# Attention laid between feed-forward matmuls: value products of a tile as one unit, and scores on four quarters of the array

## The chip, the cores and the metric

One core of a Trainium2 chip runs the kernel. The metric is the device time of one execution in microseconds, the median of several runs; lower is better.

## The reference

Three layers, one after the other. Pooled attention: keys and values are averaged over groups of 8 tokens, so each of 576 queries of a batch sees 72 keys. Then a feed-forward layer over 4608 tokens, and a mixture of 8 experts of which each token takes the best one.

```
k_p = k.reshape(B, H, 72, 8, 64).mean(axis=3); v_p likewise      # B = H = 8, D = 64
scores = scale * q @ k_p.T;  attn = exp(scores - max);  attn /= sum + 1e-9
x = (attn @ v_p), as [4608, 512]
h = x @ w_in                                                      # 512 -> 2048
g = h where h >= 1, 0 where h <= -1, else (h + 1)**2 / 4
y = g @ w_out                                                     # 2048 -> 512
e = argmax(y @ w_gate);  out = p_e * relu(y @ w1[e]) @ w2[e]      # 512 -> 1024 -> 512
```

## The kernel before

The order of the work is written out by hand; each engine runs its instructions in the order in which the code issues them.

The 4608 tokens are 36 tiles of 128, in ten blocks of 3, 4 (seven times), 3 and 2 tiles. For each block `j` the feed-forward layer makes 16 steps `m`: `f1(j, m)` (L592 to L594, 12 matmuls into bank `ps0` or `ps1`) computes 128 of the 2048 hidden columns, and `f2(j, m)` (L635 to L637, three matmuls a tile into `ps2` to `ps5`) adds their share to the output. Each product is three matmuls of a high and a low part (hi x hi, hi x lo, lo x hi). `f1` runs two steps ahead of `f2`. Between them the activation goes through DVE (clip, L599), ACT (square, L600), DVE (larger of both, L610), ACT (high part, L611), DVE (low part, L621); the last three are put off to the next `flush()` through the list `later`.

After each `f1` and each `f2` comes a `slot(j, s)`, s = 0 to 31. A slot of block `j` issues the attention of the tiles of block `j + 1`: `run_units` takes about one unit from the list `units`, then `flush()`, then one or two steps from `todo`, the routing of block `j - 1` (its logits are L666 and L672, its counts L697 and L698). To some units a `kv_step` is tied: the sum over 8 tokens of a head's keys or values on DVE (L244).

The units of a tile are listed by `tile_units`, seven of them, and `weave` mixes those of neighbouring tiles. They are: 0 the transposed queries (`u_qt`), 1 and 2 the scores of heads 0 to 3 and 4 to 7 (`u_sc`), 3 and 5 the turning of the probabilities, 4 and 6 the value products of heads 0 to 3 and 4 to 7 (`u_pv`). For tiles 9 to 33 (`turned`) 3 is `u_turn_p`, a transpose on DVE (L383, L385) and a store to `p_d`, and 5 is `u_place_p`, the loads from `p_d` into `PT` (L392); the order is 3, 2, 5, 0 of the next tile, 4, 6. Both banks that units and routing may use are `ps6` and `ps7`, handed out in turn by `bank()`.

`u_sc` computes two heads with one matmul of the whole array (L340): 128 rows are the 64 dimensions of two heads, and the 144 moving columns of `KBD` hold the pooled keys of both with zeros in the off-diagonal blocks. DVE takes the maxima (L347) and subtracts (L357), and after the second half ACT takes the exponential (L360). A tile that straddles two batches (4, 13, 22, 31) does so for 64 tokens at a time, with 64 columns of the array.

`u_pv` computes a head with one matmul (L416; 72 keys are the rows, 64 dimensions the columns, 128 tokens move), two heads for the upper and lower half of a bank. ACT writes the high part to `XT` (L421), DVE the low part (L422); `XT` is what `f1` of the next block streams.

`u_kt(b)` turns the pooled keys of a batch and writes both blocks of `KBD` (L291, L292).

Of the kernel before, what the change touches and what calls it, by code (L numbers as in the profile page):

```python
# [13 lines left out]
ALU = mybir.AluOpType  # L14
# [9 lines left out]
def attention_ffn_routed_experts_kernel(  # L24
# [38 lines left out]
    AHEAD = 2  # L63
    PICK = NB - 4
    TURN0, TURN1 = 9, NTILE - 2
    CHUNK = S // 64

    sb = ctx.enter_context(tc.tile_pool(name="sb", bufs=1))
# [35 lines left out]
    def at(o, n, p=128):  # L104
        return AT[0:p, o:o + n]
# [2 lines left out]
        return FX[:, o:o + n]  # L108

    KBD = [at(576 * i, 576).rearrange("p (a c) -> p a c", a=4) for i in range(2)]  # L110
    QB = [at(1152 + 512 * i, 512) for i in range(2)]
    QT = at(2176, 512)
    SC = [at(2688, 576), at(7616, 576)]
# [100 lines left out]
    def turned(t):  # L214
        return TURN0 <= t < TURN1
# [38 lines left out]
    def bank():  # L254
        banks.rotate(-1)
        return banks[-1]
# [6 lines left out]
    def mix(n=1):  # L263
        for _ in range(min(n, len(pend))):
            pend.popleft()()
# [19 lines left out]
    def u_kt(b):  # L285
        pb = bank()
        for c in range(4):
            nc.tensor.transpose(pb[:, c * SP_:(c + 1) * SP_], KP[:, c * 128:(c + 1) * 128],
                                ident[0:SP_, 0:SP_])
        src = pb[:, 0:4 * SP_].rearrange("p (a c) -> p a c", a=4)  # L290
        nc.scalar.activation(out=KBD[b % 2][0:64, :, 0:SP_], in_=src[0:64], func=ACTF.Copy)  # L291
        nc.scalar.activation(out=KBD[b % 2][64:128, :, SP_:2 * SP_], in_=src[64:128],  # L292
                             func=ACTF.Copy)

    smx3 = sb.tile([128, 3, H, 1], F32, name="smx3")
    ssm3 = sb.tile([128, 3, H, 1], F32, name="ssm3")
# [8 lines left out]
    def sc_of(t):  # L305
        return SCH if t == 2 else SC[t % 2]

    def sc3_of(t):
        return sc_of(t).rearrange("p (h c) -> p h c", h=H)

    def pt_of(t, hf):
        return PTX[(2 * t + hf) % 4] if t < HEAD else PT[:, hf]
# [22 lines left out]
    def u_sc(t, hf):  # L335
# [23 lines left out]
            if hf:  # L359
                nc.scalar.activation(out=sc, in_=sc, func=ACTF.Exp, scale=1.0 / 64)  # L360
        if hf:
            def rest():
                if t >= HEAD:
                    nc.vector.tensor_reduce(out=ssm, in_=sc3, axis=AX.X, op=ALU.add)
                    mix()
                nc.vector.tensor_scalar(ssm, ssm, 1e-9, None, op0=ALU.add)
                nc.vector.reciprocal(out=ssm, in_=ssm)
                if turned(t):
                    nc.vector.tensor_tensor(out=sc3, in0=sc3, op=ALU.mult,
                                            in1=ssm.to_broadcast([128, H, SP_]))  # L370
                elif t >= HEAD:
                    later.append(norm)
                else:
                    norm()

            def norm():
                nc.gpsimd.tensor_tensor(out=sc3, in0=sc3, in1=ssm.to_broadcast([128, H, SP_]),
                                        op=ALU.mult)
            later.append(rest)

    def u_turn_p(t):
        sc = sc3_of(t)
# [18 lines left out]
        nc.scalar.activation(out=pt, in_=pb[0:SP_], func=ACTF.Copy)  # L401
        mix()

    def u_pv(t, hf, xb, col):

        pb = bank()
        pt = pt_of(t, hf)
        for i in range(4):
            hd = slice((4 * hf + i) * D, (4 * hf + i + 1) * D)
            ps0, cs0 = i % 2 * 64, i // 2 * 128  # L410
            for p0, p1, b, s in segs(t):
                src = pt[:, i * 128 + p0:i * 128 + p1]
                if turned(t):
                    h = 4 * hf + i
                    src = PTB[:, p0 // 32:p1 // 32, 32 * h:32 * h + 32]
                nc.tensor.matmul(pb[ps0:ps0 + 64, cs0 + p0:cs0 + p1], VS[:, b % 2, hd], src,  # L416
                                 start=True, stop=True)
        src = pb[:, 0:256].rearrange("p (c s) -> p c s", c=2)
        ch = slice(2 * hf, 2 * hf + 2)
        hi, lo = XT[:, xb, 0, ch, col:col + 128], XT[:, xb, 1, ch, col:col + 128]  # L420
        nc.scalar.activation(out=hi, in_=src, func=ACTF.Copy, scale=0.125)  # L421
        nc.vector.scalar_tensor_tensor(out=lo, in0=src, scalar=0.125, in1=r32(hi), op0=ALU.mult,  # L422
                                       op1=ALU.subtract)
        mix()
# [31 lines left out]
    def tile_units(t):  # L456
        j, c = tile_block[t]
        a = dict(xb=j % 2, col=c * 128)
        pt = [lambda: u_pt(t, 0), lambda: u_pt(t, 1)]
        if turned(t):  # L460
            pt = [lambda: u_turn_p(t), lambda: u_place_p(t)]
        return [lambda: u_qt(t), lambda: u_sc(t, 0), lambda: u_sc(t, 1), pt[0],
                lambda: u_pv(t, 0, **a), pt[1], lambda: u_pv(t, 1, **a)]

    def weave(ta, tb):

# [639 lines left out]
    with tc.manual_schedule():  # L1106
# [9 lines left out]
        def run_units(n):  # L1116
            for _ in range(n):
                units.popleft()[1]()
            if qloads:
                qloads.popleft()()  # L1120
# [65 lines left out]
        def slot(j, s):  # L1186

            want = min(state["units"], -(-(s + 1) * state["units"] // (22 if j == NB - 2 else 29 - 2 * AHEAD + 2)))
            run_units(want - state["done"])
            state["done"] = max(want, state["done"])  # L1190
            flush()
            if j == 0:
                for _ in range(min(1, PER[s // 2]) if s % 2 == 0 else PER[s // 2] - 1):
                    tick()
                if kv:
                    kv.popleft()()
            for _ in range(2 if j >= NB - 2 else 1 + s % 2):
                if todo:
                    todo.popleft()()
            if j == PICK + 2 and s == 0:  # L1200
# [249 lines left out]
```

## Time and profile before

| | us |
|---|---|
| median of 3 runs | 1460.14 |
| lowest, highest | 1453.12, 1464.66 |
| profiled execution, its time | 1460.49 |
| profiled execution, its span | 1458.7 |

The profile is one execution, recorded by the hardware. Its page gives the busy time of each engine: PE is TensorE's matmuls, PEld its weight loads, DVE, ACT and POOL the other engines, SP the queue that issues DMAs. The other views answer questions on the trace: busy time in given stretches, groups of instructions by line and form, single instructions in order of time, and waits with what ended them.

### The profile page before, as it was taken

To read this page: it belongs to the slowest core of one execution; us is meant where nothing else is said; L and a number is where in the kernel's file an instruction comes from. 1 tells how busy PE (TensorE), PEld (TensorE's weight loads), DVE (VectorE), ACT (ScalarE), POOL (GpSimd) and SP (SyncE) were. 2 spreads that over 40 slices of the span, in tenths; PEclk is the share of its full clock that TensorE was granted. 3 is DMA by queue.
4 is the path that set the end of the run, shared out by engine and by line. 5 is a ranking of instruction groups with operands and counts; after the bars stand their busy time and mean duration, and the time that the engine had idled before them with its cause. 6 is when DMAs were issued, how large, how long until landed. Compare 5 with 4: busy or idle time off the path is not lost. (4 is left out here: it accounts for less than half of the span.)

```text
span 1458.7 us, 20361 instructions
## 1 busy us (share of the span) xinstructions
PE 1396.6 (96%) x7296; PEld 1127.7 (77%) x7296; DVE 864.4 (59%) x1725; ACT 423.0 (29%) x784; POOL 183.0 (13%) x206
## 2 busy tenths in 40 slices
PE   6799988999999999999999999998989999999897
PEld 5666777777887878878778788887878888888785
DVE  4679879767777865976875546455432333322435
ACT  5344332322222222232222223243111111111334
POOL 3152000001001000010010011111322112111211
PEclk9899999999999999999999999999999999999999
DMA  8566557446446454563653344571543223332504
GB/s 232 146 210 183 160 154 215 160 122 194 135 139 175 142 174 123 155 187 119 165 170 106 103 138 126 182 265 61 183 132 97 85 80 116 102 101 71 183 30 152
DMA packets 170824, 210.63 MB, mean 144 GB/s; under 512 B 84199, under 2 KB 114055, under 8 KB 170696
## 3 DMA queue, kind: packets, MB, share of 16 engines
q1 hardware_dynamic: 136120, 103.74, 24.4%
q10 hardware_dynamic: 26784, 83.96, 17.7%
q0 software_dynamic: 7792, 21.35, 4.7%
q8 instruction: 64, 1.05, 0.3%
q14 instruction: 64, 0.52, 0.1%
HBM read 182.93 MB, written 49.66 MB: 159 GB/s over the span
## 5 line engine op out<-in xcount | busy, mean ns | idle before, releaser
L592 PE MATMUL ps<-XT,W 128*128 128x512 f32 (+2 forms) x640 | 247.5, 387 | 2.2 <-DVE FG L621 2.1
L593 PE MATMUL ps<-XT,W 128*128 128x512 f32 (+2 forms) x640 | 238.2, 372 | 1.6 <-DVE XT L422 1.6
L594 PE MATMUL ps<-XT,W 128*128 128x512 f32 (+2 forms) x640 | 237.7, 371 | 0.0
L600 ACT ACTIVATE FX<-FX,half 128x512 f32<-128x512 f32 (+2 forms) x152 | 104.0, 684 | 426.2 <-DVE FX L599 394.1
L635 PE MATMUL ps<-WO,FG 128*128 128x512 f32 x528 | 216.4, 410 | 0.0
L636 PE MATMUL ps<-WO,FG 128*128 128x512 f32 x528 | 208.0, 394 | 0.0
L637 PE MATMUL ps<-WO,FG 128*128 128x512 f32 x528 | 207.3, 393 | 0.0
L599 DVE TENSOR_SCALAR FX<-ps 128x512 f32<-128x512 f32 (+2 forms) x152 | 96.6, 636 | 99.4 <-PE ps L594 99.2
L997 DVE SCALAR_TENSOR_TENSOR FG<-ps,FG 128x512 fp32r<-128x512 f32 (+1 forms) x64 | 43.2, 674 | 181.3 <-ACT FG L996 181.2
L592 PEld LDWEIGHTS ps<-XT,W 128*128 128x128 f32 x640 | 121.7, 190 | 27.1 <-issue 4.5
L593 PEld LDWEIGHTS ps<-XT,W 128*128 128x128 f32 x640 | 121.9, 190 | 19.7 <-DVE XT L422 2.3
L594 PEld LDWEIGHTS ps<-XT,W 128*128 128x128 f32 x640 | 121.7, 190 | 18.6
L728 POOL DMA_INDIRECT perm_d<-idt,POSI x36 | 35.3, 982 | 726.5 <-DVE SM L714 594.7
L611 ACT ACTIVATE FG<-ps 128x512 fp32r<-128x512 f32 (+2 forms) x144 | 81.1, 563 | 154.5 <-DVE ps L610 133.2
L610 DVE TENSOR_TENSOR ps<-FX,ps 128x512 f32<-128x512 f32 (+2 forms) x144 | 92.8, 644 | 44.7 <-ACT FX L600 44.7
L635 PEld LDWEIGHTS ps<-WO,FG 128*128 128x128 f32 x528 | 99.9, 189 | 24.5 <-issue 5.4
L637 PEld LDWEIGHTS ps<-WO,FG 128*128 128x128 f32 x528 | 99.8, 189 | 22.5
L636 PEld LDWEIGHTS ps<-WO,FG 128*128 128x128 f32 x528 | 100.2, 190 | 17.6
L996 ACT ACTIVATE FG<-ps 128x512 fp32r<-128x512 f32 (+1 forms) x64 | 37.4, 585 | 249.2 <-PE ps L993 235.5
L621 DVE TENSOR_TENSOR FG<-ps,FG 128x512 fp32r<-128x512 f32 (+2 forms) x144 | 91.3, 634 | 27.9 <-ACT FG L611 27.8
L991 PE MATMUL ps<-XT,W 128*128 128x512 f32 (+1 forms) x256 | 99.0, 387 | 2.4 <-ACT XT L975 2.4
L992 PE MATMUL ps<-XT,W 128*128 128x512 f32 (+1 forms) x256 | 99.3, 388 | 0.5 <-DVE XT L976 0.2
(235 smaller groups left out, 2228.8 us busy)
## 6 DMA issues: line engine op xcount, KB each, us to landing
WO<-wo_d ACTq DMA_DIRECT2D x128, 512.0 KB
AT<-in_moe_w_dram SPq DMA_DIRECT2D x10, 2048.0 KB
AT<-in_moe_w_dram SPq DMA_DIRECT2D x14, 1024.0 KB
p_d<-AT SPq DMA_DIRECT2D x25, 384.0 KB
AT<-in_v_dram SPq DMA_DIRECT2D x60, 144.0 KB
wo_d<-WO SPq DMA_DIRECT2D x16, 512.0 KB
AT<-in_k_dram SPq DMA_DIRECT2D x56, 144.0 KB
yrow_d<-Y ACTq DMA_DIRECT2D x7, 1032.0 KB
```

The lines of the kernel that those rows point to most:

```text
L592: nc.tensor.matmul(o, wi(m, 0, c), xh, start=(c == 0), stop=False)
L593: nc.tensor.matmul(o, wi(m, 0, c), xl, start=False, stop=False)
L594: nc.tensor.matmul(o, wi(m, 1, c), xh, start=False, stop=(c == KD - 1))
L599: nc.vector.tensor_scalar(r, o, -1.0, 1.0, op0=ALU.max, op1=ALU.min)
L600: nc.scalar.activation(out=r, in_=r, func=ACTF.Square, scale=0.5, bias=half)
L610: nc.vector.tensor_tensor(out=o, in0=r, in1=o, op=ALU.max)
L621: nc.vector.tensor_tensor(out=gl, in0=o, in1=r32(gh), op=ALU.subtract)
L635: nc.tensor.matmul(o, gh, WO[:, g % 4, 0], start=(m == 0), stop=False)
L636: nc.tensor.matmul(o, gh, WO[:, g % 4, 1], start=False, stop=False)
L637: nc.tensor.matmul(o, gl, WO[:, g % 4, 0], start=False, stop=(m == KF - 1))
L991: nc.tensor.matmul(o, e1(0)[:, c, ms], xh, start=(c == 0), stop=False)
L992: nc.tensor.matmul(o, e1(0)[:, c, ms], xl, start=False, stop=False)
```

## The change

From tile 3 on (`JOIN`) the value products of a tile are one unit: unit 4 is empty, and unit 6 issues all eight heads into one bank, then one ACT and one DVE instruction of 512 columns.

From tile 9 on (`TURN0`) the scores are one unit, `u_sc_all`: unit 1 is empty, and unit 2 issues 16 matmuls, each for one head and 64 tokens. Head `2c + i` uses the 64 rows from `64 i`, tokens 64 to 127 (`g` = 1) the columns from 64; even heads go to one bank, odd ones to the other. The keys stand in `KB` without zero blocks, so 72 columns move, and `u_kt` writes them with one ACT instruction. DVE makes a maximum and a subtraction for each bank. A straddling tile needs nothing of its own, since 64 tokens lie in one batch. `wide` tells the slot that it held such a unit; it then takes no routing step (in blocks before the last two). What follows the scores (`rest`, `norm`) moves into `finish` as it was.

```diff
+    JOIN = 3
...
+    KB = [at(576 * i, 4 * SP_).rearrange("p (a c) -> p a c", a=4) for i in range(2)]
...
         src = pb[:, 0:4 * SP_].rearrange("p (a c) -> p a c", a=4)
-        nc.scalar.activation(out=KBD[b % 2][0:64, :, 0:SP_], in_=src[0:64], func=ACTF.Copy)
-        nc.scalar.activation(out=KBD[b % 2][64:128, :, SP_:2 * SP_], in_=src[64:128],
-                             func=ACTF.Copy)
+        nc.scalar.activation(out=KB[b % 2], in_=src, func=ACTF.Copy)
+
+    wide = [False]
+
+    def u_sc_all(t):
+        pbs = [bank(), bank()]
+        for c in range(4):
+            for g in range(2):
+                toks = slice(64 * g, 64 * g + 64)
+                kb = KB[(t * 128 + 64 * g) // S % 2]
+                for i in range(2):
+                    rows = slice(64 * i, 64 * i + 64)
+                    nc.tensor.matmul(pbs[i][toks, c * SP_:(c + 1) * SP_],
+                                     QT[rows, c * 128 + 64 * g:c * 128 + 64 * g + 64],
+                                     kb[rows, c], start=True, stop=True)
+        sc, sc3, smx = sc_of(t), sc3_of(t), smx3[:, t % 3]
+        for i in range(2):
+            src = pbs[i][:, 0:4 * SP_].rearrange("p (h c) -> p h c", h=4)
+            hs = slice(i, H, 2)
+            nc.vector.tensor_reduce(out=smx[:, hs], in_=src, axis=AX.X, op=ALU.max)
+            mix()
+            nc.vector.tensor_tensor(out=sc3[:, hs], in0=src,
+                                    in1=smx[:, hs].to_broadcast([128, 4, SP_]), op=ALU.subtract)
+        nc.scalar.activation(out=sc, in_=sc, func=ACTF.Exp, scale=1.0 / 64)
+        wide[0] = True
+        finish(t)
...
-    def u_pv(t, hf, xb, col):
-
+    def u_pv(t, halves, xb, col):
         pb = bank()
-        pt = pt_of(t, hf)
-        for i in range(4):
-            hd = slice((4 * hf + i) * D, (4 * hf + i + 1) * D)
-            ps0, cs0 = i % 2 * 64, i // 2 * 128
+        for h in range(4 * halves[0], 4 * halves[-1] + 4):
+            ps0, cs0 = h % 2 * 64, (h // 2 - 2 * halves[0]) * 128
             for p0, p1, b, s in segs(t):
-                src = pt[:, i * 128 + p0:i * 128 + p1]
+                src = pt_of(t, h // 4)[:, h % 4 * 128 + p0:h % 4 * 128 + p1]
                 if turned(t):
-                    h = 4 * hf + i
                     src = PTB[:, p0 // 32:p1 // 32, 32 * h:32 * h + 32]
-                nc.tensor.matmul(pb[ps0:ps0 + 64, cs0 + p0:cs0 + p1], VS[:, b % 2, hd], src,
-                                 start=True, stop=True)
-        src = pb[:, 0:256].rearrange("p (c s) -> p c s", c=2)
-        ch = slice(2 * hf, 2 * hf + 2)
+                nc.tensor.matmul(pb[ps0:ps0 + 64, cs0 + p0:cs0 + p1],
+                                 VS[:, b % 2, h * D:(h + 1) * D], src, start=True, stop=True)
+        n = 2 * len(halves)
+        src = pb[:, 0:n * 128].rearrange("p (c s) -> p c s", c=n)
+        ch = slice(2 * halves[0], 2 * halves[0] + n)
...
-        return [lambda: u_qt(t), lambda: u_sc(t, 0), lambda: u_sc(t, 1), pt[0],
-                lambda: u_pv(t, 0, **a), pt[1], lambda: u_pv(t, 1, **a)]
+        sc = [lambda: u_sc(t, 0), lambda: u_sc(t, 1)]
+        if t >= TURN0:
+            sc = [lambda: None, lambda: u_sc_all(t)]
+        pv = [lambda: u_pv(t, [0], **a), lambda: u_pv(t, [1], **a)]
+        if t >= JOIN:
+            pv = [lambda: None, lambda: u_pv(t, [0, 1], **a)]
+        return [lambda: u_qt(t), *sc, pt[0], pv[0], pt[1], pv[1]]
...
+            wide[0] = False
             run_units(want - state["done"])
...
-            for _ in range(2 if j >= NB - 2 else 1 + s % 2):
+            for _ in range(2 if j >= NB - 2 else 0 if wide[0] else 1 + s % 2):
```

The order of the instructions, before and after, at three places. A number ahead of a row counts the engine's instructions; `x2` means that a row stands that often in a row. `ps_73` and `ps_74` are the banks of `f1`, `ps_75` to `ps_78` those of `f2`, `ps_79` and `ps_80` the two free ones; `AT` holds queries, keys and scores. Lines after the change stand 32 further on (L592 is L624, L635 is L667).

TensorE around the second score half of tile 14, before (the first half, of the same kind, stands 23 rows earlier):

```order
939 L636 MATMUL ps_78<-WO,FG 128x512
940 L637 MATMUL ps_78<-WO,FG 128x512
941 L340 MATMUL ps_80<-AT 128x144 x2
942 L592 MATMUL ps_73<-XT,W 128x512
943 L593 MATMUL ps_73<-XT,W 128x512
```

TensorE around the end of the score unit of tile 14, after:

```order
1011 L305 MATMUL ps_80<-AT 64x72
1012 L305 MATMUL ps_79<-AT 64x72
1013 L305 MATMUL ps_80<-AT 64x72
1014 L305 MATMUL ps_79<-AT 64x72
1015 L305 MATMUL ps_80<-AT 64x72
1016 L624 MATMUL ps_73<-XT,W 128x512
1017 L625 MATMUL ps_73<-XT,W 128x512
```

Twice two matmuls on the whole array, in two places of the program, have become sixteen in one place (rows 1000 to 1015, all of this kind), the banks in turn.

DVE over the two score halves of tile 13, before (L383 and L385 are the turning of the tile ahead, L658 is routing):

```order
406 L599 TENSOR_SCALAR FX<-ps_74 128x512
407 L347 TENSOR_REDUCE smx_126<-ps_79 128x4
408 L357 TENSOR_TENSOR AT<-ps_79,smx_126 128x288
409 L610 TENSOR_TENSOR ps_74<-FX,ps_74 128x512
410 L658 STREAM_TRANSPOSE WG<-Y 128x512
411 L383 STREAM_TRANSPOSE AT<-AT 128x8x2x32
412 L385 STREAM_TRANSPOSE AT<-AT 128x256
413 L621 TENSOR_TENSOR FG<-ps_74,FG 128x512
414 L599 TENSOR_SCALAR FX<-ps_73 128x512
415 L347 TENSOR_REDUCE smx_126<-ps_80 128x4
416 L357 TENSOR_TENSOR AT<-ps_80,smx_126 128x288
417 L610 TENSOR_TENSOR ps_73<-FX,ps_73 128x512
```

DVE at the scores of the same tile after (L312 and L314 are the maxima and the subtraction of `u_sc_all`):

```order
400 L653 TENSOR_TENSOR FG<-ps_74,FG 128x512
401 L690 STREAM_TRANSPOSE WG<-Y 128x512
402 L631 TENSOR_SCALAR FX<-ps_73 128x512
403 L312 TENSOR_REDUCE smx_126<-ps_80 128x4
404 L314 TENSOR_TENSOR AT<-ps_80,smx_126 128x4x72
405 L312 TENSOR_REDUCE smx_126<-ps_79 128x4
406 L314 TENSOR_TENSOR AT<-ps_79,smx_126 128x4x72
407 L642 TENSOR_TENSOR ps_73<-FX,ps_73 128x512
```

The pair that stood ahead of one larger-of (L610) now stands with the other pair ahead of the next one (L642), and no routing step follows in that slot.

DVE over the two value halves of tile 11, before:

```order
401 L422 SCALAR_TENSOR_TENSOR XT<-ps_79,XT 128x2x128
402 L610 TENSOR_TENSOR ps_73<-FX,ps_73 128x512
403 L658 STREAM_TRANSPOSE WG<-Y 128x512
404 L422 SCALAR_TENSOR_TENSOR XT<-ps_80,XT 128x2x128
405 L621 TENSOR_TENSOR FG<-ps_73,FG 128x512
```

And of the same tile after:

```order
391 L631 TENSOR_SCALAR FX<-ps_73 128x512
392 L642 TENSOR_TENSOR ps_73<-FX,ps_73 128x512
393 L449 SCALAR_TENSOR_TENSOR XT<-ps_79,XT 128x4x128
394 L653 TENSOR_TENSOR FG<-ps_73,FG 128x512
395 L690 STREAM_TRANSPOSE WG<-Y 128x512
```

The first half is gone from its slot, and the low part of all four columns of heads is written in the slot of the second half.

## Rows read from the trace of the kernel before

**Rows 1.** The page, busy us (share of the span), instructions, of two engines.

```profile
PE 1396.6 (96%) x7296; PEld 1127.7 (77%) x7296; DVE 864.4 (59%) x1725; ACT 423.0 (29%) x784; POOL 183.0 (13%) x206
```

**Rows 2.** Two stretches: length, busy time of each engine, granted clock, DMA share, GB/s.

```profile
core 0: us, PE busy (x) PEld busy (x) DVE busy (x) ACT busy (x) POOL busy (x), PEclk, DMA share, GB/s
185.00:290.00 105.00, 96.56 (x485) 77.89 (x484) 84.30 (x154) 33.86 (x63) 3.56 (x3) 0.95 0.59 179
...
500.00:600.00 100.00, 100.00 (x545) 79.31 (x544) 69.61 (x139) 27.13 (x47) 3.83 (x4) 1.00 0.50 148
```

**Rows 3.** PE's groups by line and form: rows*columns of the array, xcount, busy, mean ns.

```profile
L340 PE MATMUL ps<-AT 128*128 128x144 f32 x248 | 42.9, 299 | 8.3 <-ACT AT L331 5.5 <-DVE AT L357 2.8
L416 PE MATMUL ps<-PT,VS 72*64 72x128 f32 x464 | 38.7, 290 | 7.2 <-DMA PT<-p_d 6.2 <-ACT PT L401 0.9
```

**Rows 4.** PE's timeline at a score half: start us, length us, line, form, xcount.

```profile
328.05 0.39 PE L636 MATMUL ps<-WO,FG 128*128 128x512 f32 x1
328.28 0.39 PE L637 MATMUL ps<-WO,FG 128*128 128x512 f32 x1
328.50 0.65 PE L340 MATMUL ps<-AT 128*128 128x144 f32 x4
328.90 0.49 PE L592 MATMUL ps<-XT,W 128*128 128x512 f32 x1
329.22 0.40 PE L593 MATMUL ps<-XT,W 128*128 128x512 f32 x1
```

**Rows 5.** PE's timeline at a value half.

```profile
315.15 0.39 PE L637 MATMUL ps<-WO,FG 128*128 128x512 f32 x1
315.47 0.66 PE L416 MATMUL ps<-PT,VS 72*64 72x128 f32 x8
316.06 0.50 PE L592 MATMUL ps<-XT,W 128*128 128x512 f32 x1
316.40 0.40 PE L593 MATMUL ps<-XT,W 128*128 128x512 f32 x1
```

**Rows 6.** PE's timeline at a score half of a straddling tile and routing's logits.

```profile
305.19 0.71 PE L340 MATMUL ps<-AT 128*64 128x144 f32 x8
305.83 1.08 PE L666 MATMUL ps<-WG 128*32 128x128 f32 x32
306.84 0.50 PE L635 MATMUL ps<-WO,FG 128*128 128x512 f32 x1
```

**Rows 7.** PE's timeline at a pooling of two heads' keys (L279).

```profile
60.62 1.22 PE L279 MATMUL ps<-ident,AT 72*64 72x72 f32 x32
61.77 0.45 PE L592 MATMUL ps<-XT,W 128*128 128x384 f32 x1
```

**Rows 8.** PE's timeline where both value halves stand in one slot.

```profile
229.49 0.39 PE L594 MATMUL ps<-XT,W 128*128 128x512 f32 x1
233.34 1.97 PE L416 MATMUL ps<-PT,VS 72*64 72x128 f32 x16 [3.46 <-DMA PT<-p_d]
235.24 0.80 PE L635 MATMUL ps<-WO,FG 128*128 128x512 f32 x1
```

**Rows 9.** Groups of DVE and ACT by line and form.

```profile
L599 DVE TENSOR_SCALAR FX<-ps 128x512 f32<-128x512 f32 x112 | 76.7, 685 | 72.0 <-PE ps L594 71.9
L621 DVE TENSOR_TENSOR FG<-ps,FG 128x512 fp32r<-128x512 f32 x112 | 75.8, 677 | 16.1 <-ACT FG L611 16.0
L244 DVE TENSOR_REDUCE VS<-AT 72x64 f32<-72x512 f32 x50 | 52.2, 1044 | 0.0
...
L347 DVE TENSOR_REDUCE smx<-ps 128x4 f32<-128x288 f32 x72 | 32.1, 446 | 20.6 <-PE ps L340 20.6
L422 DVE SCALAR_TENSOR_TENSOR XT<-ps,XT 128x256 fp32r<-128x256 f32 x72 | 30.3, 422 | 65.4 <-ACT XT L421 65.4
L357 DVE TENSOR_TENSOR AT<-ps,smx 128x288 f32<-128x288 f32 x66 | 30.2, 457 | 2.2
...
L611 ACT ACTIVATE FG<-ps 128x512 fp32r<-128x512 f32 x112 | 67.1, 599 | 136.5 <-DVE ps L610 116.9 <-DVE MX L684 8.5 <-DVE CB L700 7.1
```

**Rows 10.** PE's waits from 100 to 900 us: us in total, times, longest.

```profile
PE ps L416 <- DMA PT<-p_d: 6.2, 5, 3.5
...
PE ps L592 <- DVE FG L621: 0.3, 1, 0.3
```

More of the change, by code (lines that the diff above doesn't have):

```diff
@@ L361, in u_sc, with finish, rest, norm @@
         if hf:
[L362 to L379, printed above, removed]
+            finish(t)
+    def finish(t):
+        sc3, ssm = sc3_of(t), ssm3[:, t % 3]
+        def rest():
+            if t >= HEAD:
+                nc.vector.tensor_reduce(out=ssm, in_=sc3, axis=AX.X, op=ALU.add)
+                mix()
+            nc.vector.tensor_scalar(ssm, ssm, 1e-9, None, op0=ALU.add)
+            nc.vector.reciprocal(out=ssm, in_=ssm)
+            if turned(t):
+                nc.vector.tensor_tensor(out=sc3, in0=sc3, op=ALU.mult,
+                                        in1=ssm.to_broadcast([128, H, SP_]))
+            elif t >= HEAD:
+                later.append(norm)
+            else:
+                norm()
+        def norm():
+            nc.gpsimd.tensor_tensor(out=sc3, in0=sc3, in1=ssm.to_broadcast([128, H, SP_]),
+                                    op=ALU.mult)
+        later.append(rest)
     def u_turn_p(t):
```

## The prediction

> **What bounds the kernel now.** I read the page's busy times first, then the windows, the forms by line, a few stretches of TensorE's timeline, and the waits. The reader is to see one engine without air: PE is busy 96% of the span, DVE 59% [rows 1], and between 500 and 600 us PE is busy the whole 100 us at the full granted clock [rows 2]. So, while the feed-forward layer runs with the attention of the next tiles laid between its matmuls, time is what PE's stream takes. An attention unit costs what it pushes the next feed-forward matmul back, and work of DVE or ACT costs nothing unless PE waits for it.
>
> I measure a unit's price so: from the start of the last 512-column matmul before it to the start of the second one after it, less two regular steps of 0.23 us (328.05 to 328.28 [rows 4]). (The second, since the first one after a unit of smaller tiles runs long, 0.50 us instead of 0.39 [rows 4, 5].) A score half of one batch: 328.28 to 329.22 is 0.94, less 0.46 = 0.48 us [rows 4]. It is four records (an fp32 matmul leaves two) of 144 columns on the whole array, 0.12 us each, 0.83 ns a column, and nothing over: it enters and leaves for free. A value half: 315.15 to 316.40 is 1.25, less 0.46 = 0.79 us [rows 5]. Its eight records of 128 columns would stream 8 x 0.107 = 0.85 us one after the other, more than the 0.59 us from its first start to the next line's. So the two column halves of the array run at the same time, 4 x 0.107 = 0.43 us, and the other **0.36 us is entering and leaving** the small tiles (0.16 of it inside the 0.59, 0.20 outside). A tile that straddles two batches has score halves of eight records on 64-column tiles: 4 x 0.12 + 0.36 = 0.84 us, and 305.19 to 305.83 is 0.64, plus 0.20 outside, the same 0.84 [rows 6].
>
> **The change part by part.** Durations are of the profiled execution, 1460.49 us with a span of 1458.7; the median shown is 1460.14, so no correction is needed between them.
>
> Value products as one unit, tiles 3 to 35, 33 tiles: the streams stay, one entering and leaving of 0.36 us goes. One tile had both halves in one slot already (16 records at 233.34 [rows 8]), so 32 x 0.36 = **-11.5 us**. The matmuls of the two straddling halves only grow in number with the same columns, so they save the same. One eviction of 512 columns on ACT and DVE replaces two of 256; by [rows 9] DVE spends 422 ns on a half and 677 ns on 512 columns, so it sheds about 0.17 us a tile, beside PE, worth nothing. It ends later than a half did: the next block's first matmul comes 12 matmuls, 2.8 us, after the last value unit, and ACT and DVE need about 0.60 + 0.69 plus the queue. I cost that at nothing; without the cover it is some 0.5 us at each of eight block ends, 4 us.
>
> Scores as one unit, tiles 9 to 35, 27 tiles. Now 16 matmuls of 64 rows by 64 columns with 72 moving columns, 32 records. Nothing in the trace uses half the rows of the array (scores now take 128 rows, value products 72 [rows 3]), so the price has two ends. If the four corners run at once, eight groups of 72 x 0.83 = 0.06 us stream 0.48 us, and the unit, which now enters and leaves small tiles like a value unit, costs 0.48 + 0.36 = 0.84 us. If every record runs alone, it is 32 x 0.06 + 0.36 = 2.28 us. I take 0.84: pairs with these very 72 columns do run together, 32 records in 1.15 us from 60.62 to 61.77 [rows 7], where one by one would be 1.92; and four column tiles run together at L666, 32 records of 128 columns in 1.01 us, where pairs would need 1.71 [rows 6]. For 24 tiles of one batch the price was 2 x 0.48 = 0.96, so 24 x -0.12 = -2.9 us. The three straddling tiles (13, 22, 31) cost 2 x 0.84 and now no more than the others: 3 x -0.84 = -2.5 us. Together **-5.4 us**.
>
> Waits. From 100 to 900 us PE waits 6.2 us in five places for the turned probabilities to land [rows 10]. The unit that waits is the first value half; joined, the work stands where the second half stood, a slot or more later. That takes the wait from four, and leaves the longest, 3.5 us, where both halves had been in one slot: **-2.7 us**.
>
> New waits. The score unit takes both free banks, so PE needs both evicted before it, and DVE gets its two maxima and two subtractions in a row: 2 x 446 + 2 x 457 ns = 1.81 us [rows 9]. Queued behind them on DVE stand the steps of the feed-forward activation (the larger-of, the low part), for which a later f1 or f2 waits. Before, half of that came in a slot. The cover is that these results are used two steps of some 5.5 us on, and that routing steps are left out of a slot with scores; PE's present waits for the low part are 0.3 us in this stretch [rows 10]. Bounds: 0, and 27 x 0.7 = 19 us (third rival). I take **+1.0 us**, near that row.
>
> Sum: -11.5 - 5.4 - 2.7 + 1.0 = -18.6; 1460.5 - 18.6 = **1441.9, say 1442 us**, 1.3% below. What follows the attention (the routed experts) keeps its order and moves forward with it.
>
> **The rivals.**
>
> First, four at a time doesn't pay in full: the rows of the array take turns, or records cannot follow each other faster than anywhere now. For it: no run of 32 records in the trace passes in less than 1.01 us [rows 6], and half-row tiles are new. Against it: those runs are set by their columns, 128 or 72, not by their number. Price: 1.01 to 1.15 inside plus 0.20, 1.21 to 1.35 us a tile; 24 x (+0.25 to +0.39) is 6.0 to 9.4, three straddling tiles give -1.4 to -1.0; with the other terms -8.6 to -4.8, so 1452 to 1456. The Trainium skill, TensorE: Matmul & The Clock Gate, section "Wait — 56ns, not 53.3ns?", says that starts of matmuls never come closer than about 25 ns however small they are; by it 32 records would take 0.80 us and the sum about 1450. The trace does not decide it: its fastest long run has 32 ns per record from [rows 6].
>
> Second, the slower side: no overlap of the corners at all. The place is the score unit, the price 2.28 us: 24 x 1.32 + 3 x 0.60 = 33.5, less 11.5 and 2.7, plus 1.0, is +20.3: 1481 us. It decides from where the unit costs more than its present mean of 1.04 by (11.5 + 2.7 - 1.0) / 27 = 0.49, so from 1.53 us no gain is left, and from 2.07 us the kernel is over 1% slower. Against it stands [rows 7], where pairs already halve the time: for this even the column halves would have to lose what they have.
>
> Third, DVE holds PE up: in a slot with the score unit DVE may have 1.81 of scores, 1.04 of key and value sums and 0.69 of the activation's clip [rows 9], 3.54 us against a slot of 12 x 0.23 = 2.76. If 0.7 us of it reached PE at all 27 tiles, that is 19 us, 1461, no change. For it: DVE is busy 84 of 105 us between 185 and 290 us [rows 2]. Against it: later it is busy 70%, and the slack of two steps.
>
> **How the numbers follow.** Forecast 0.62 (1436 to 1448 by itself: the lower end if the 3.5 us wait goes with the stretch at lower clock behind it and no wait comes, the upper if block ends lose their cover); first rival 0.21; third 0.10; second 0.07. A measurement can tell about 1% of this kernel from no change, 14.6 us. The forecast lies 4 us beyond that, so I give a little over four fifths of it to faster: 0.52, and 0.03 from mixed cases of the first rival: 0.55. Same is the rest of the forecast, most of the first rival and the third: 0.37. Slower is the second and a little of the third: 0.08. The range reaches from 1434, a little under the forecast's own end as single runs before differ by some us, to 1465, over the first and third rivals; the second is left out.
>
> **What would show it.** After the change a score unit should be 32 records whose starts span about 0.5 us, a price of 0.84 by the measure above; 1.2 or more means the first rival, over 2 the second. A joined value unit of 16 records should cost 0.79 + 0.43 = 1.22. PE's wait for PT should be a single one of some 3.5 us, and PE's waits for DVE should stay under 2 us in all from 100 to 900 us. PE's busy time should fall by some 15 us. If units cost what I say and the time doesn't fall, the sum's frame is wrong: then PE was not what ended last.

## The result, and the profile after

| us | before | after |
|---|---|---|
| median | 1460.86 (8 runs) | 1446.71 (8 runs) |
| lowest, highest | 1453.12, 1467.25 | 1441.33, 1448.83 |
| profiled execution | 1460.49 | 1442.14 |
| its span | 1458.7 | 1440.4 |

The ratio is 0.9896, with an interval of 0.9877 to 0.9914: the kernel is 1.0% faster, 14.2 us by the medians. By the two profiled executions it is 18.3 us. The page after, in the columns of [rows 1]:

```profile
PE 1377.1 (96%) x7920; PEld 1114.1 (77%) x7920; DVE 862.5 (60%) x1692; ACT 418.3 (29%) x745; POOL 183.5 (13%) x206
```

TensorE has 624 records more and is busy 19.5 us less. The groups that stand where [rows 3] stood, with the new scores first and the turned value products after them:

```profile
L305 PE MATMUL ps<-AT 64*64 64x72 f32 x864 | 19.7, 229 | 0.0
...
L442 PE MATMUL ps<-PT,VS 72*64 72x128 f32 x464 | 31.7, 279 | 3.9 <-DMA PT<-p_d 3.4 <-ACT PT L431 0.6
```

A score unit is 32 of the 864 records, so 27 units are busy 19.7 us, 0.73 us each. The same 464 value records are busy 31.7 us instead of 38.7: they stand closer together. TensorE's timeline at a score unit after (start us, length us, line, form, count), to be laid beside [rows 4]:

```profile
400.56 0.39 PE L669 MATMUL ps<-WO,FG 128*128 128x512 f32 x1
400.88 0.73 PE L305 MATMUL ps<-AT 64*64 64x72 f32 x32
401.54 0.50 PE L624 MATMUL ps<-XT,W 128*128 128x512 f32 x1
401.88 0.40 PE L625 MATMUL ps<-XT,W 128*128 128x512 f32 x1
```

By the prediction's measure the unit costs 401.88 - 400.56 - 0.46 = 0.86 us. And at a joined value unit, for [rows 5]:

```profile
531.45 0.39 PE L669 MATMUL ps<-WO,FG 128*128 128x512 f32 x1
531.77 1.09 PE L442 MATMUL ps<-PT,VS 72*64 72x128 f32 x16
532.79 0.50 PE L624 MATMUL ps<-XT,W 128*128 128x512 f32 x1
533.13 0.40 PE L625 MATMUL ps<-XT,W 128*128 128x512 f32 x1
```

533.13 - 531.45 - 0.46 = 1.22 us for both halves, where two apart took 1.58. TensorE's waits from 100 to 900 us after (us in all, times, longest), for [rows 10]:

```profile
PE ps L442 <- DMA PT<-p_d: 3.4, 4, 1.7
PE ps L624 <- DVE FG L653: 2.3, 3, 1.2
PE ps L365 <- DVE AT L382: 2.1, 2, 1.5
...
PE ps L624 <- ACT XT L448: 0.9, 1, 0.9
PE ps L429 <- DVE XT L449: 0.9, 1, 0.9
```

The wait for the turned probabilities falls from 6.2 to 3.4 us. The longest of before, 3.5 us at 233 us [rows 8], is still the longest, with 1.7 us at 230.5. Against it stand new waits: 2.3 us for the low part of the activation (L653, 0.3 before), 0.9 us for the high part of a value unit (L448), at the start of block 1. L365 and L429 stand before 150 us, at tiles that keep their scores. The window that in [rows 2] had a granted clock of 0.95 (columns as there) now reads:

```profile
185.00:290.00 105.00, 97.61 (x596) 77.61 (x596) 86.11 (x156) 34.52 (x60) 3.12 (x3) 0.97 0.61 182
```

In this execution no stretch at the lower clock follows that wait any more: from 228 to 242 us the granted clock is 1.00, where it was 0.76. In a second execution of the same kernel ("After, a second time") it is 0.88, so how much of it is the change's stays open.

To see where the time went, take the start of the first `f1` matmul of each block (L592, now L624) in the timeline. Before, blocks 2, 4, 6 and 8 start at 266.0, 468.1, 668.7 and 866.7 us, the experts' first product (L991, now L1023) at 995.0, and the span ends at 1458.7. Each kernel of this study stands against that so (us, profiled executions; the names are those of the next section):

| kernel | block 2 | block 4 | block 6 | block 8 | experts | end |
|---|---|---|---|---|---|---|
| after | -4.2 | -8.8 | -13.5 | -18.1 | -18.6 | -18.3 |
| after, second time | -3.6 | -9.1 | -13.8 | -18.4 | -18.9 | -18.4 |
| values only | -5.3 | -10.2 | -13.5 | -16.9 | -17.4 | -18.3 |
| scores only | -2.4 | 5.9 | 6.1 | 6.3 | 7.7 | 9.1 |
| corner by corner | -4.4 | -3.0 | -0.9 | 0.2 | 0.5 | 2.0 |
| rows in turn | -4.2 | -3.8 | -6.5 | -9.6 | -9.8 | -9.1 |
| no skip | -5.5 | -10.3 | -11.5 | -12.5 | -12.9 | -11.4 |
| values in two banks | -6.1 | -8.6 | -12.2 | -16.3 | -16.3 | -11.3 |
| whole array | -6.7 | -11.3 | -14.9 | -18.7 | -19.2 | -14.3 |
| values early | -2.3 | 0.6 | -2.7 | -6.3 | -6.8 | -3.3 |
| late rows | -2.8 | -9.3 | -13.9 | -18.5 | -19.0 | -15.4 |
| late rows, second time | -2.6 | -7.6 | -12.2 | -16.9 | -17.3 | -10.3 |
| scores, late rows | 4.1 | 8.4 | 7.6 | 6.3 | 6.5 | 6.7 |

After the change the gain grows evenly, some 2.3 us a block, while attention is laid between the feed-forward matmuls, and stays as it is through the experts. The last column moves by several us where nothing there was changed; so experiments are compared at the experts' start.

### The profile page after: what moved, and what is told of

Same layout as the page of the kernel before. It is cut to its first block, busy times and chain, and to the rows that moved or that the text cites. A ratio compares the mean times of both kernels' runs of the same rounds, so it can differ in the third digit from the quotient of the medians.

```text
span 1440.4 us, 21554 instructions
## 1 busy us (share of the span) xinstructions
PE 1377.1 (96%) x7920; PEld 1114.1 (77%) x7920; DVE 862.5 (60%) x1692; ACT 418.3 (29%) x745; POOL 183.5 (13%) x206
## 3 DMA queue, kind: packets, MB, share of 16 engines
q10 hardware_dynamic: 26784, 83.96, 18.1%
## 5 line engine op out<-in xcount | busy, mean ns | idle before, releaser
L624 PE MATMUL ps<-XT,W 128*128 128x512 f32 (+2 forms) x640 | 246.0, 384 | 4.8 <-DVE FG L653 3.6
L667 PE MATMUL ps<-WO,FG 128*128 128x512 f32 x528 | 211.4, 400 | 0.4 <-DMA WO<-wo_d 0.4
L668 PE MATMUL ps<-WO,FG 128*128 128x512 f32 x528 | 207.1, 392 | 0.0
L669 PE MATMUL ps<-WO,FG 128*128 128x512 f32 x528 | 206.4, 391 | 0.0
L624 PEld LDWEIGHTS ps<-XT,W 128*128 128x128 f32 x640 | 121.3, 190 | 31.5 <-DVE FG L653 6.0
L642 DVE TENSOR_TENSOR ps<-FX,ps 128x512 f32<-128x512 f32 (+2 forms) x144 | 92.9, 645 | 58.7 <-ACT FX L632 57.7
L667 PEld LDWEIGHTS ps<-WO,FG 128*128 128x128 f32 x528 | 99.7, 189 | 23.2 <-issue 2.4
L668 PEld LDWEIGHTS ps<-WO,FG 128*128 128x128 f32 x528 | 99.7, 189 | 18.3
L653 DVE TENSOR_TENSOR FG<-ps,FG 128x512 fp32r<-128x512 f32 (+2 forms) x144 | 91.8, 638 | 35.2 <-ACT FG L643 33.7
L1023 PE MATMUL ps<-XT,W 128*128 128x512 f32 (+1 forms) x256 | 98.7, 386 | 2.9 <-ACT XT L1007 2.9
```

What stands on the lines that cost most here:

```text
L624: nc.tensor.matmul(o, wi(m, 0, c), xh, start=(c == 0), stop=False)
L642: nc.vector.tensor_tensor(out=o, in0=r, in1=o, op=ALU.max)
L653: nc.vector.tensor_tensor(out=gl, in0=o, in1=r32(gh), op=ALU.subtract)
L667: nc.tensor.matmul(o, gh, WO[:, g % 4, 0], start=(m == 0), stop=False)
L668: nc.tensor.matmul(o, gh, WO[:, g % 4, 1], start=False, stop=False)
L669: nc.tensor.matmul(o, gl, WO[:, g % 4, 0], start=False, stop=(m == KF - 1))
```

## The experiments

The theory: a unit costs its streams plus 0.36 us for entering and leaving small tiles; joining saves the second 0.36, and four corners of the array run at once. The rivals: the corners take turns, or DVE and the banks hold TensorE up. Every kernel below computes all that the reference asks for. The corner-by-corner, rows-in-turn, whole-array and values-early kernels have a single run each, so they are compared by their profiles.

**Values alone.** The scores as before, the value products joined:

```diff
-        if t >= TURN0:
-            sc = [lambda: None, lambda: u_sc_all(t)]
```

> Value products as one unit alone, scores as before. My sum: 32 x 0.36 us of entering and leaving and 2.7 us of waits for PT go, so 14 us off a run of before, ratio about 0.990, and a joined unit priced at 1.22 us. If the gain came from the scores or only from both together, it would be under 5 us.

Measured: 1451.62 us median (1442.24 to 1455.67 in 7 runs), 0.9927 of before (0.9902 to 0.9953). The unit is 1.22 us as after. At the experts' start its profile has 17.4 of the 18.6 us; but that execution was the fastest of the seven, so the medians (8.9 of 14.2 us) and the profiles disagree on how much is left to the scores: 1 to 5 us.

**Scores alone.** The value halves apart (`JOIN = NTILE`), the scores as after.

> Scores as one unit alone, value products in halves as before. My sum: 24 x 0.12 + 3 x 0.84 = 5.4 us off, less about 1 us of new waits, ratio about 0.997; score units at 0.86 us, PE's waits for PT still there (about 6 us). If the score unit's burst on DVE and its two banks held PE up, the ratio would be 1.00 or more, with waits of f1 and of the next unit for DVE.

Measured: 1468.32 us (1465.29 to 1469.5 in 6 runs), 1.0051 of before (1.0034 to 1.0068). It is slower, though each score unit costs the same 0.86 us. TensorE's waits, 100 to 960 us:

```profile
PE ps L442 <- DMA PT<-p_d: 11.6, 6, 3.3
...
PE ps L442 <- DVE G L734: 2.1, 1, 2.1
...
PE ps L442 <- DVE AT L314: 1.1, 1, 1.1
...
PE ps L442 <- ACT WG L700: 0.9, 2, 0.5
```

The first value half (L442) now waits 11.6 us for its probabilities, and 4.1 us for banks that routing (L734, L700) or the scores (L314) still hold. Then the clock; three windows around two of the waits (columns as in [rows 2]):

```profile
350.00:357.00 7.00, 5.71 (x26) 4.39 (x24) 6.90 (x12) 1.54 (x3) 1.01 (x2) 1.00 0.91 298
357.00:365.00 8.00, 6.30 (x22) 4.62 (x23) 2.44 (x4) 0.98 (x2) 0.91 (x1) 0.57 0.42 126
...
463.00:471.00 8.00, 6.82 (x28) 4.98 (x28) 3.19 (x6) 0.98 (x2) 0.96 (x1) 0.57 0.62 147
```

At 358.70 TensorE has waited 2.99 us, and in the 8 us around it the granted clock is 0.57, which is most of them at the lower level of 1.2 GHz. What that costs shows beside the same unit of tile 10, which waited 2.64 us and kept the full clock. In both places twelve feed-forward matmuls stand between this value half and the next:

```profile
256.60 0.66 PE L442 MATMUL ps<-PT,VS 72*64 72x128 f32 x8 [2.64 <-DMA PT<-p_d]
...
260.13 0.66 PE L442 MATMUL ps<-PT,VS 72*64 72x128 f32 x8
...
358.70 1.12 PE L442 MATMUL ps<-PT,VS 72*64 72x128 f32 x8 [2.99 <-DMA PT<-p_d]
...
364.94 0.66 PE L442 MATMUL ps<-PT,VS 72*64 72x128 f32 x8
```

At full clock that is 3.53 us, at the lower 6.24, so 2.7 us more. Of the three long waits of this kernel (2.6, 3.0 and 3.3 us) two were followed by the lower clock and cost nearly twice their length, and one was not. The saving on the units (-4.9) is less than the waits and the clock take.

**Corner by corner.** The 16 matmuls of a score unit in another order, all four of a corner behind one another:

```diff
-        for c in range(4):
-            for g in range(2):
-                toks = slice(64 * g, 64 * g + 64)
-                kb = KB[(t * 128 + 64 * g) // S % 2]
-                for i in range(2):
-                    rows = slice(64 * i, 64 * i + 64)
+        for g in range(2):
+            toks = slice(64 * g, 64 * g + 64)
+            kb = KB[(t * 128 + 64 * g) // S % 2]
+            for i in range(2):
+                rows = slice(64 * i, 64 * i + 64)
+                for c in range(4):
```

> The same sixteen matmuls, but the four of one quarter of the array follow each other. If overlap needs neighbours in the order on different quarters, 32 records of 0.06 us run one by one: 1.92 + 0.36 = 2.28 us a unit instead of 0.86, and 27 x 1.42 = 38 us more than the changed kernel. If TensorE finds the overlap whatever the order, the unit stays at 0.86 us.

Measured: 1462.42 us in one run. Its score group and one unit in the timeline:

```profile
L305 PE MATMUL ps<-AT 64*64 64x72 f32 x864 | 44.0, 229 | 0.0
```

```profile
405.17 0.39 PE L669 MATMUL ps<-WO,FG 128*128 128x512 f32 x1
405.49 1.63 PE L305 MATMUL ps<-AT 64*64 64x72 f32 x32
...
407.39 0.40 PE L625 MATMUL ps<-XT,W 128*128 128x512 f32 x1
```

44.0 us instead of 19.7, and 407.39 - 405.17 - 0.46 = 1.76 us a unit. The corners run at once only if neighbours in the stream belong to different corners. It is not the 2.28 us of no overlap: the single records start 62 ns apart within a corner, and around each of the three changes of corner some of both run side by side. By price that is 27 x 0.90 = 24.3 us; its profile is 19.1 us behind the change at the experts' start, and of the difference its shorter waits and 3.4 us less at the lower clock make up some 4.

**Rows in turn.** The halves of the rows one after the other, the halves of the columns still in turn (`for i`, then `c`, then `g`).

> The same sixteen matmuls, first the eight of the upper row half (left and right in turn), then those of the lower half, so only two quarters alternate. If two quarters overlap and no more, 16 x 0.06 + 0.36 = 1.32 us a unit, 27 x 0.46 = 12 us more than the changed kernel; if TensorE looks ahead over eight matmuls, 0.86 us.

Measured: 1451.34 us in one run:

```profile
L305 PE MATMUL ps<-AT 64*64 64x72 f32 x864 | 27.8, 229 | 0.0
```

```profile
405.25 0.39 PE L669 MATMUL ps<-WO,FG 128*128 128x512 f32 x1
...
406.87 0.40 PE L625 MATMUL ps<-XT,W 128*128 128x512 f32 x1
```

By the timeline a unit costs 406.87 - 405.25 - 0.46 = 1.16 us, between the 0.86 of four at once and the 1.32 of pairs; here too the records overlap at the one change. It is the pairs of [rows 7] that one gets without the row halves, so those are worth 0.30 us a unit. 27 x 0.30 = 8.1; its profile is 8.8 us behind at the experts' start.

**No skip.** Routing steps stay in the slots with a score unit:

```diff
-            for _ in range(2 if j >= NB - 2 else 0 if wide[0] else 1 + s % 2):
+            for _ in range(2 if j >= NB - 2 else 1 + s % 2):
```

> The changed kernel, but a slot with scores takes its routing steps as before. In the traces so far the left-out steps put the 1 MB store of routing's rows (512 packets of 2064 bytes, 345.7 to 350.7 us) on top of the store of the turned probabilities (348.7 to 351.8), whose loads into PT then issue 8.3 us after it instead of 4.1 (tiles 10, 14, 18, 26, 30), and PE waits for PT. Theory: without the skip that gap goes back to some 4 us, PE's waits for PT fall below 3.4 us, and the time is 2 to 5 us under the changed kernel. Rival: the skip is needed, since DVE's burst of scores and routing steps holds PE up; then PE's waits for DVE rise by several us and the time is above the changed kernel's.

Measured: 1451.77 us (1448.34 to 1456.91 in 9 runs), 0.9939 (0.9918 to 0.996), some 5 us behind the change. TensorE's waits, 100 to 960 us:

```profile
PE ps L698 <- DVE AT L314: 6.5, 3, 2.7
...
PE ps L305 <- DVE G L734: 2.2, 1, 2.2
...
PE ps L305 <- ACT WG L700: 1.1, 2, 0.6
```

Routing's logits (L698) wait for the subtraction of a score unit that holds their bank, and score units wait for routing. Without the skip the third rival's wait is there, in a few places rather than at all 27 tiles. The first half of the theory came true: SP waits 38.9 us in all for the stores of the probabilities, where it waits 52.4 after the change (the lines stand under "Late rows"), and TensorE 2.6 us instead of 3.4 for the loads. The time does not follow it.

**After, a second time**, unchanged.

> The changed kernel once more. Its executions lie between 1441 and 1449 us and the profiled one, at 1442, is near the lower end. If the spread comes from waits for PT and the stretches at the lower clock behind them, a profiled execution above 1445 us shows more of both at tiles 10, 14 and 18; if it comes from elsewhere (experts, the end), the blocks up to 920 us agree with the first profile within 1 us.

Measured: 1443.83 us (1441.95 to 1445.73 in 4 runs), 0.9885 (0.9856 to 0.9913); its blocks start within 0.8 us of those of the first profile, from block 3 on within 0.4. The gain in the stretch that was changed repeats. The profiled execution is the fastest of its four, so it can't tell what makes the longer ones longer. TensorE's waits from 100 to 900 us:

```profile
PE ps L442 <- DMA PT<-p_d: 2.2, 4, 1.6
...
PE ps L624 <- DVE FG L653: 1.1, 2, 0.8
```

Each of the two is 1.2 us less than in the first profile. Yet after its wait at 230.94 us the clock falls, and from 150 to 960 us it has 10.2 us at the lower clock, as much as before the change, where the first profile has 6.8. So waits and clock differ by amounts like these between two executions of one kernel whose blocks start together.

**Values in two banks.** Both halves in the one slot, but each with its own bank and eviction:

```diff
-            pv = [lambda: None, lambda: u_pv(t, [0, 1], **a)]
+            pv = [lambda: None, lambda: [u_pv(t, [0], **a), u_pv(t, [1], **a)]]
```

> The changed kernel, but the two value halves, both in the later slot, keep a bank and an ACT and a DVE instruction each. If the gain of the joined unit is the entering and leaving of small tiles once instead of twice, the unit is still priced at 1.22 us and the time equals the changed kernel's within 0.3%. If it came from one eviction instead of two, it is 5 us or more slower.

Measured: 1447.54 us (1447.32 to 1449.08 in 4 runs), 0.9905 (0.9877 to 0.9933). The unit costs the same 1.22 us: the gain is in entering and leaving, not in the wider eviction. What the one bank spares shows in the waits, 100 to 960 us:

```profile
PE ps L704 <- DVE XT L449: 2.2, 3, 1.2
PE ps L442 <- DVE G L734: 2.1, 1, 2.1
PE ps L729 <- DVE XT L449: 1.8, 3, 0.6
```

Routing (L704, L729) waits for the second bank, and once the second value half for a bank that routing holds (L734); at the experts' start this is 2.3 us behind the change.

**Whole array.** One score unit in one place and two banks, but with the matmuls of before (128 rows, 144 columns with the zero blocks).

> The changed kernel, but the score unit makes before's four matmuls of 144 columns on the whole array (eight on 64 columns where a tile straddles), 2 heads each, in the two banks. Same burst on DVE, same skip. By the prices: 0.96 us instead of 0.86 a unit, 1.3 to 1.7 for three straddling tiles, so 24 x 0.1 + 3 x 0.6 = 4 us above the changed kernel, and the waits for PT as there.

Measured: 1446.08 us in one run. Its unit in the timeline:

```profile
398.66 0.39 PE L669 MATMUL ps<-WO,FG 128*128 128x512 f32 x1
...
400.11 0.40 PE L625 MATMUL ps<-XT,W 128*128 128x512 f32 x1
```

A unit costs 0.99 us, 0.13 more than on quarters, and a straddling tile 1.33. Yet it stands at -19.2 at the experts' start, no worse than the change: its wait for the probabilities is

```profile
PE ps L442 <- DMA PT<-p_d: 1.2, 1, 1.2
```

from 100 to 900 us, 2.2 us less than in the first profile of the change and 1.0 less than in the second, and it has 3.4 us at the lower clock instead of 6.8 and 10.2. The 3 to 5 us that the quarters save by price are within what waits and clock make; that the quarters save time is so not shown, and this one run doesn't say which is better.

**Values early.** The joined value unit in the place of the first half (unit 4) for the turned tiles:

```diff
-            pv = [lambda: None, lambda: u_pv(t, [0, 1], **a)]
+            pv = [lambda: u_pv(t, [0, 1], **a), lambda: None]
+            if not turned(t):
+                pv.reverse()
```

> The changed kernel, but for the turned tiles the joined value unit stands where the first half stood (one slot or two earlier). Theory: scores alone were 7.5 us slower than before because that first place comes before PT has landed, and the join hides it by its later place; then PE's waits for PT go up from 3 to 10 us or more here, with stretches at the lower clock behind them, and the time is 10 us or more above the changed kernel's. Rival: the place doesn't matter, the time stays within 3 us of 1442 to 1447.

Measured: 1457.1 us in one run. Its waits, 100 to 960 us, begin with

```profile
PE ps L442 <- DMA PT<-p_d: 12.4, 8, 3.6
```

and at 253 to 261 us its granted clock is 0.57. Of 18.6 us only 6.8 are left at the experts' start. So the place is worth 12 us: the joined unit in the later slot is what gives the turned probabilities time to land, and what hides the same lateness that "scores alone" lays open.

**Late rows.** That lateness has a cause on the queues. SP's queue around tile 14, before (start us, length us, line; L386 stores the turned probabilities, L392 loads them back):

```profile
349.63 0.40 SPq L386 DMA_DIRECT2D p_d<-AT  x1
350.12 3.51 SPq L238 DMA_DIRECT2D AT<-in_k_dram  x2
353.74 1.17 SPq L392 DMA_DIRECT2D PT<-p_d  x3
```

And after (L416 the store, L422 the load):

```profile
343.99 1.23 SPq L416 DMA_DIRECT2D p_d<-AT  x1
345.32 3.07 SPq L240 DMA_DIRECT2D AT<-in_k_dram  x2
352.30 1.36 SPq L422 DMA_DIRECT2D PT<-p_d  x3
```

From store to load it is 4.1 us before, 8.3 after. In between, after, ACT's queue issues routing's store of a block's rows (1 MB, at 342.8 us), whose packets run from 345.7 to 350.7 us; the packets of the probabilities land from 348.7 to 351.8. This kernel puts that store five routing steps later:

```diff
         if j < NB - 2:
+            st.extend([lambda: None] * 5)
             st.append(store_rows)
```

> The changed kernel with routing's row store five steps (some three slots) later, so that it no longer starts within 2 us of the store of tile 14, 18, 26 or 30's probabilities. Theory: the loads into PT then issue 4 to 5 us after that store instead of 7 to 8 at tiles 14, 26 and 30; PE's waits for PT fall from 3.4 us to about the 1.7 of tile 9, and the time is 1 to 4 us under the changed kernel's. Rival: the gap between store and loads has another cause and stays at 7 to 8 us.

Measured: 1442.28 us (1439.61 to 1447.1 in 6 runs), 0.9869 (0.9839 to 0.9899). SP's wait for the store from 180 to 860 us, of after and then of this kernel:

```profile
SPq L422 <- DMA p_d<-AT: 52.4, 16, 7.1
```

```profile
SPq L422 <- DMA p_d<-AT: 36.7, 16, 4.3
```

So the collision is real and gone (35.9 us in all before the change). TensorE gets little of it: its wait for the probabilities is 3.0 us, within the 3.4 and 2.2 of the change's two profiles. Those at tiles 14 and 16 are gone, and one of 1.4 us at tile 10 has come; the second profile of this kernel has 2.5 us, 0.9 of it at tile 16. The experts start 0.4 us earlier.

**Scores alone with late rows**, both edits.

> Scores alone as one unit (value products in halves), with the row store five steps later. Theory: the 11.6 us of PE's waits for PT in the scores-only kernel come from that store; they fall to some 4 us, and the time from 1468 to 1457 or less, that is under before, as the prices of the units say. Rival: they come from DVE's burst ahead of the turning; then waits and time stay.

Measured: 1466.59 us (1459.49 to 1470.13 in 10 runs), 1.0023 (0.9999 to 1.0047). TensorE waits 7.9 us in 4 places, not 11.6 in 6; those of tiles 10, 14 and 18 stay, at 1.9 to 2.9 us. The theory that the row store makes "scores alone" slow holds for a third of that wait; the banks (4.0 us) and the lower clock stay. What makes the others late was not tried.

**Late rows, a second time.**

> The kernel with the late row store once more, to see whether it beats the changed kernel as well as the one before. If it does, its ratio stays at 0.987 or under and its median at 1443 us or under; if the first result was a lucky draw, it comes out at 0.989 and 1444 to 1447 us, like the changed kernel.

Measured: 1445.05 us (1438.17 to 1450.11 in 6 runs), 0.988 (0.9853 to 0.9906). Both times it is faster than the kernel before by more than its interval, and neither time can it be told from the change; the 0.9869 of the first time was at least in part a lucky draw. Its profiled execution was its longest, with a span of 1448.4 us, and shows where executions of one kernel differ. A window at the start, of the first time and then of this one (columns as in [rows 2]):

```profile
15.00:60.00 45.00, 30.54 (x224) 24.62 (x223) 29.07 (x60) 23.75 (x82) 13.32 (x18) 0.81 0.76 205
```

```profile
15.00:60.00 45.00, 34.45 (x184) 26.86 (x183) 28.32 (x57) 22.93 (x80) 13.11 (x17) 0.66 0.74 204
```

The granted clock is 0.66 instead of 0.81 there, and TensorE is 2.5 us later at block 1. The attention's blocks then pass as in the other profile, and the experts lose 7.0 us against before's experts (-17.3 to -10.3), where the first time lost 3.6. TensorE's waits from 1340 to 1460 us are 10.1 us in all against 8.9, in part at other places, so they account for about 1 of these 3.4 us.

## Why the prediction was right, and where it was off

The forecast of 1442 us was right in its sign, and in its mechanism for the value products; 1446.7 lies in the range and in the forecast's own 1436 to 1448. For the scores the price of the unit was right, but that it saves time is not shown. At 14.2 us the gain lies just under the 14.6 that the prediction set between faster and same, so of its chances the 0.37 for same applies and not the 0.55 for faster, though the interval is clear of no change. By its steps:

- **What bounds.** The frame holds: TensorE's time in the stream is what counts. It is busy 19.5 us less (some 15 were expected), and the span is 18.3 us shorter.
- **Joined value products, -11.5.** Right. 1.22 us was predicted and 1.22 measured, 0.36 less than two halves, at 32 tiles. That it is the entering and leaving is shown by the two-bank kernel with the same 1.22; two straddling halves (0.86 each by the same measure) became 1.33. The later eviction, put at nothing, costs 1.1 us at the start of block 1 (0.9 for L448 and 0.2 for L449) and nothing at the other block starts.
- **Scores, -5.4.** Near: the unit is 0.86, not 0.84 us, so 24 x -0.10 and 3 x -0.82 make -4.9. The two kernels with another order show that it is the four corners at once. But as a term of the sum it doesn't stand alone: by itself the edit costs 7.8 us, without it 17.4 of the 18.6 us are there in the profile, and with the whole array in its place the time is about the same.
- **Waits for the probabilities, -2.7.** The size is right (6.2 to 3.4), its working only in part, and that the errors cancel is luck. The wait of [rows 8], which was to stay at 3.5 us, fell to 1.7: TensorE is ready for the unit 1.1 us earlier (228.4 instead of 229.5 us), and the loads have landed 2.9 us earlier (230.5 instead of 233.3). Instead of none at the other tiles, three of 0.2 to 0.8 us remain, one of them at a tile that had none. The reason given, the later place, holds. What was missed is that the change also brings the loads later against their stores (SP waits 52.4 us for these instead of 35.9): in the earlier place the joined unit pays 12.4 us ("values early"), twice the 6.2 of before, so the term hangs on the place more than the prediction knew.
- **New waits, +1.0.** Too low. From 150 to 960 us TensorE's waits for DVE and ACT rise from 1.1 to 5.0 us, 2.4 of it for the low part of the activation that the prediction saw queued behind the scores (0.3 to 2.7; 1.0 with the values alone, 1.5 in the change's second profile). The criterion of under 2 us for DVE from 100 to 900 us failed: 5.5, where before had 2.3. The row from which the 1.0 was taken, 0.3 us, was of an order with half of the scores' DVE work in a slot.
- **Not in the sum:** 10.2 us at the lower clock between 150 and 960 us became 6.8, worth at most 1.7. With the measured terms the sum is -11.5 - 4.9 - 2.8 + 3.9 - 1.7 = -17.0; 18.6 were measured at the experts' start. In the change's second profile the terms are -11.5 - 4.9 - 4.0 + 2.7, with the clock as before: -17.7, of 18.9 measured. So 1.6 and 1.2 us are not assigned, and that the forecast's -18.6 is met to the tenth by the first profile is luck: waits that were put too low stand against clock and a rest that were not in the sum.
- **The step that missed the median by 4.7 us** is the first one of the sum, that no correction is needed between a profiled execution and the median. Before, the two agree within 0.4 us; after, the profiled execution is 4.6 us under the median, the second fastest of eight, and the second profile is the fastest of its four. Those of its runs above 1447 us had a mean granted clock of 0.981 to 0.984, the two fastest 0.984 and 0.987. The late-rows profile shows such a difference in the first 60 us and in the experts; why the executions spread so, and why both profiles of the change fell on the fast side, was not found.

The first rival (1452 to 1456) falls with the unit's 0.86 us. The rule that was weighed for it, from the Trainium skill, TensorE: Matmul & The Clock Gate, section "Wait — 56ns, not 53.3ns?", that starts never come closer than about 25 ns, doesn't hold here: 32 records start between 400.88 and 401.54 us, at most 21 ns apart in the mean, and the single records of a group of four start 6 to 7 ns apart. The Trainium skill, TensorE: Matmul & The Clock Gate, section "The mechanism", has tiles at different positions start about 4 ns apart, and that is near what the trace shows. The second rival (1481) falls too; the order of the matmuls decides how near one comes to it. The third, DVE and the banks, is the one that took something: 3.9 us as the change stands, some 5 more by the medians without the skip.

## What to carry to other kernels

Between matmuls of the whole array each group of small tiles has an entry price (0.36 us here), so groups should be joined, and within one the stream should change the corner with every matmul. Price an edit together with the place that it gives to a unit: the same joined unit one place earlier lost 12 of 18.6 us to a transfer that had been hidden, and the other edit, cheaper by every unit, was slower alone. When a sum of a few us is met by one profile, compare a second profile of the same kernel and the other runs, before a wait is credited to the change or the head and the tail of the program are called unchanged.

## What the runs showed of the hardware

- Matmuls on four 64 x 64 corners run four at a time in fp32: 32 records of 72 columns cost 0.86 us in alternating order, 1.16 with the rows in turn, 1.76 corner by corner. Where a run of one corner ends, some records of the next join in, which makes 1.76 out of 2.28 and 1.16 out of 1.32.
- In "scores alone" a wait of TensorE of 2.99 us was followed by 6.8 us at the lower clock (357 to 365 us, granted 0.57), which cost 2.7 us, nearly as much again as the wait; one of 3.26 us was followed by the same, and one of 2.64 us by none.
- A store of 1 MB on ACT's queue put off the landing of a small one on SP's queue: the load behind that one was issued 8.3 us after the store instead of 4.1, and 4.9 with the large one moved.
